# The order of loads, clamps, exponentials and score products in the head of an attention and MLP kernel, and one clamp further on

## The chip, the core and the metric

The kernel runs on one NeuronCore of a Trainium2 chip. The core has five engines with queues of their own, each of which works through its instructions in order: TensorE (PE, matrix products; PEld is its weight load), VectorE (DVE), ScalarE (ACT), GpSimd (POOL) and SyncE (SP, which here issues nearly all DMAs). They meet through semaphores. The metric is the device time of one execution in microseconds (us), less being better; the kernel before takes 689.08 us, the median of three runs (689.06 to 689.25).

## The reference

x is 8 x 8 x 512 x 64 (batch, head, position, depth), state 8 x 8 x 32 x 64. A softmax reads the state from every position of x, another reads x from every state row; both results, side by side along the sequence, go through an MLP of width 2048 with a sigmoid-approximated GELU.

```python
scores = scale * np.matmul(x, state.transpose(0, 1, 3, 2))
a = softmax(scores)                      # with max subtracted and 1e-9 added to the sum
xread = np.matmul(a, state)
scores2 = scale * np.matmul(state, x.transpose(0, 1, 3, 2))
a2 = softmax(scores2)
sread = np.matmul(a2, x)
x = concat([xread, sread], axis=2)       # -> 4352 tokens x 512
h = x @ w_in                             # 512 x 2048
g = h * (1.0 / (1.0 + np.exp(-1.702 * h)))
return g @ w_out                         # 2048 x 512
```

(`softmax` and `concat` stand for lines written out in the reference.) All arrays are float32, but the two weights are handed over as float64.

## The kernel before

The weights' 64-bit words are loaded as they are and turned into float32 on the core, in pieces of 128 x 512 numbers: 16 pieces of w_in (piece 4c+k is the k-th block of 128 rows of column block c), then 16 of w_out. So w_in's third and fourth pieces are pieces 2 and 3, needed for the first column block; w_out's fifth is piece 20 (`nin + 4`). A piece takes these steps:

- `mask` (L221, DVE): the exponent bits of the high words.
- `round_a`: clamps the exponent to float32's range and scales it: two Relu activations on ACT (L232, L233), or for pieces 18 and 19 two `tensor_scalar` on DVE (L229, L230).
- `fraction` (L239, DVE), `sign` (L245, DVE, needs the clamped exponent), then L258 and L264 on DVE, the last writing the float32 piece.

`powers_to(n)` runs `round_a` up to piece n; `piece(fill)` finishes the next piece and puts `fill` between its two last steps; `round_to(n, ahead)` finishes all pieces up to n, each with clamps of the following ones.

The order of all work is written by hand: each engine gets its instructions in the order in which the program issues them. The head (L1295 to L1369) treats batches 0 and 1. SP's loads are issued in the order state (on ACT), pieces 0 and 1, batch 0's x in four parts, piece 2, batch 1's x in two halves (into the tile `sums`), then pieces 3 and up. Eight DMA semaphores go round, so from the ninth load on an issue waits for the landing of the one eight places before.

For each batch the head does the following. `two_states` (PE) and `state_copies` (ACT) transpose the state. `xT_part(b, j)` transposes two heads' x on PE (L356) and copies them on ACT (L357); parts 0 and 1 use x's first half, parts 2 and 3 its second. `att_scores` (L444) makes the scores of all 512 positions: for head row j, group g and half i, a 64-row by 32-column product on the array's tile given by i (rows) and j (columns), written to banks `o_0` and `o_1`. `score_copies` (ACT, L363) moves them to SBUF, `scores_back` (PE, L372) turns them, for batch 0 into the banks `held`. `head_max` and `head_sub` (DVE, L379 and L386) subtract each maximum, `head_exp` (ACT, L390) is one activation over 1024 elements a partition, `head_sum` (L402 to L405) and `head_scale` (L413) normalize on DVE, `head_back` (PE L422, ACT L423) turns back to `aT`.

`att_M` (PE L430, copied on ACT at L566) multiplies w_in's column block by the state: the state's reading and w_in become one matrix M, so that the nonlinear half is GELU of M times `aT` (`up_x`, PE L655, tile h; GELU at L644). The first `up_x` needs column block 0, that is pieces 0 to 3, and batch 0's normalized exponentials.

Much later, at 73 to 86 us, the product with w_out begins (L1552 on). It uses seven products P1 to P7 in place of eight. In the first pass (i = 0), pieces up to 17 are made, P1, second reads and M's of both batches are done, P2, one product of `up_x(1, f_early)` whose GELU goes to xn's place, `att_srT`, then `pair_sums` (sums on DVE, L1469), `round_to(nin + 4)` (pieces 18 and 19, with piece 20's clamp on ACT), `powers_to(nin + 6)`, P6 and the rest. P7 and P3 use the two banks of tile tag `h`, which the GELU of `up_x(1, f_early)` and one before must have read.

Of the kernel before, what the change touches and what calls it, by code (L numbers as in the profile page):

```python
# [20 lines left out]
def kernel(  # L21
# [194 lines left out]
    def mask(i):  # L216

        _, hi = words(i)
        sc = low[:, 2 + i % (AHEAD + 1)].bitcast(I32)
        power[i] = sc  # L220
        nc.vector.tensor_scalar(sc, hi, 0x7FF00000, None, ALU.bitwise_and)  # L221

    def round_a(i):

        if i not in power:
            mask(i)
        sc = power[i]
        if i in (NFC * NPR + 2, NFC * NPR + 3):
            nc.vector.tensor_scalar(sc, sc, most, least, ALU.min, ALU.max)  # L229
            nc.vector.tensor_scalar(sc, sc, -least, 8.0, ALU.add, ALU.mult)  # L230
            return
        nc.scalar.activation(out=sc.bitcast(FP32), in_=sc, func=AF.Relu, bias=edge[0], scale=-8.0)  # L232
        nc.scalar.activation(out=sc, in_=sc.bitcast(FP32), func=AF.Relu, bias=edge[1], scale=-1.0)  # L233

    def fraction(i):

        key = PIECES[i]
        dst = w_in[key[1]][:, key[2]] if key[0] == "i" else w_out[:, key[1]]
        nc.vector.tensor_scalar(dst.bitcast(I32), words(i)[1], 0xFFFFF, 0x100000, ALU.bitwise_and, ALU.bitwise_or)  # L239
        begun[i] = dst  # L240
# [32 lines left out]
    def load_weights(upto):  # L273
        while done["load"] < min(upto, len(PIECES)):
            load_weight(done["load"])
            done["load"] += 1

    def powers_to(n):
        while done["a"] < min(n, len(PIECES)):
            load_weights(done["a"] + 1)  # L280
            round_a(done["a"])
            done["a"] += 1
# [15 lines left out]
    def piece(fill):  # L298

        i = done["b"]  # L300
        powers_to(i + 1)
        round_b(i, i + 1, False, fill)
        done["b"] += 1
        refill()
# [27 lines left out]
    def state_copies(b):  # L332
        for t, ps in zip(A[b]["two"], A[b]["turn"]):
            nc.scalar.copy(t, ps)
# [10 lines left out]
    def xT_part(b, j, bank=None):  # L345

        if j == 0:
            A[b]["xT"] = apool.tile([P, H, 2, P], FP32, tag="xT", name=f"xT_{b}")
        h = slice(NG * j, NG * (j + 1))
        if bank is None:  # L350
            ps = att_ps([P, NG, 2, P], f"xT_{b}_{j}")
        else:
            ps = bank.rearrange("p (g i q) -> p g i q", g=NG, i=2)
        for g in range(NG):
            for i in range(2):
                nc.tensor.transpose(ps[:, g, i], x_pair(b, NG * j + g, i), ident)  # L356
        nc.scalar.copy(A[b]["xT"][:, h], ps)  # L357
# [8 lines left out]
    def scores_back(b, i, bank):  # L366

        ps = bank.rearrange("p (k g m) -> p k g m", k=2, g=NG)
        for k in range(2):
            for g in range(NG):  # L370
                o = P * (2 * g + k)
                nc.tensor.transpose(ps[:, k, g], A[b]["s"][i][:, o : o + P], ident)  # L372

    def head_max(b, i, banks):
        a = A[b]
        if i == 0:
            a["e1"] = apool.tile([P, SCH, NG, NPR, Ns], FP32, tag="e1", name=f"e1_{b}")
            a["mx"] = apool.tile([P, NG, NB], FP32, tag="mx", name=f"mx_{b}")
        nc.vector.reduce_max(out=a["mx"][:, i], in_=banks[i].rearrange("p (k n) -> p k n", n=Ns), axis=AX.X)  # L379

    def head_sub(b, i, banks):
        a = A[b]
        t = a["e1"].rearrange("p (k i) g j n -> p i k (g j) n", i=2)[:, i]
        ps = banks[i].rearrange("p (k m n) -> p k m n", k=2, n=Ns)
        mx = a["mx"][:, i].rearrange("p (k m) -> p k m", k=2)
        nc.vector.tensor_tensor(out=t, in0=ps, in1=mx.to_broadcast((P, 2, NB // 2, Ns)), op=ALU.subtract)  # L386

    def head_exp(b):
        t = A[b]["e1"]
        nc.scalar.activation(out=t, in_=t, func=AF.Exp, scale=scale)  # L390

    def head_sum(b, *fills):
# [39 lines left out]
    def att_scores(b):  # L432
        a = A[b]
        a["s"] = bank_o[:NG] if b < 2 else bank_o[NG:]
        if b > 1:
            by_state(b, a["s"], lambda rows, j: a["xT"][rows, j])
            return

        for g in range(NG):
            for j in range(NPR):  # L440
                st = slice(Ns * j, Ns * (j + 1))
                for i in range(2):
                    rows = slice(D * i, D * (i + 1))
                    nc.tensor.matmul(  # L444
                        a["s"][i][st, 2 * P * g : 2 * P * (g + 1)], state_of(b, NG * j + g, i),
                        a["xT"][rows, NG * j + g], start=True, stop=True,
                    )
# [120 lines left out]
    def att_M(b, c, spare=False, banks=None, copied=True):  # L568

        m = mpool.tile([P, NG, FC], FP32, tag=f"M{turns['M'] % NFC if b < 2 else c}", name=f"M_{b}_{c}")  # L570
        turns["M"] += 1
        A[b]["M", c] = m
        name = f"M_{b}_{c}_"
        ps = banks or [
            psH.tile([P, FC], FP32, tag="h", name=name + str(g)) if spare else att_ps([P, FC], name + str(g)) for g in range(NG)
        ]
        by_state(b, ps, lambda rows, j: w_in[c][rows, j])
        M_banks[b, c] = ps
        if copied:
            M_copies(b, c)  # L580
# [714 lines left out]
    load_two_states()  # L1295
    load_weights(2)
    load_x(0)
    load_weights(3)
    load_x(1)
    load_weights(2 * NPR)  # L1300
    nc.scalar.activation(out=one, in_=one, func=AF.Exp)
# [8 lines left out]
    keep_warm(3, held[0])  # L1310
    for j in range(NPR):
        xT_part(0, j, apart[j - 2] if j > 1 else None)
    piece(lambda: mask(2))
    powers_to(3)
    att_scores(0)
    fraction(2)
    score_copies(0)
    two_states(1, [apart[i][:, :P] for i in range(2)])
    state_copies(1)
    xT_part(1, 0)  # L1320
    scores_back(0, 0, held[0])
    piece(None)
    head_max(0, 0, held)
    mask(3)
    head_sub(0, 0, held)
    xT_part(1, 1)
    apart = [psH.tile([P, FC], FP32, tag="h", name=f"apart_{i}") for i in (2, 3)]
    xT_part(1, 2, apart[0])
    xT_part(1, 3, apart[1])
    scores_back(0, 1, held[1])  # L1330
    powers_to(NPR)
    att_scores(1)
    head_max(0, 1, held)
    fraction(3)
    head_sub(0, 1, held)
    score_copies(1)
    head_exp(0)
    apart = [psH.tile([P, FC], FP32, tag="h", name=f"apart_{i}") for i in (4, 5)]
    for i in range(2):
        scores_back(1, i, apart[i])  # L1340
# [120 lines left out]
    def pieces(t, *shape):  # L1461
        n, k = shape
        return t.rearrange("p a b -> p (a b)").rearrange("p (n k t) -> p n k t", n=n, k=k)
# [7 lines left out]
    def four(t):  # L1471
        return t.rearrange("p a b -> p (a b)").rearrange("p (n t) -> p n t", t=HS)
# [80 lines left out]
    for i in range(HF):  # L1553
        round_to(nin + 2 * i + 2)
        gelus(len(waiting))
        if i == 3:
            nc.scalar.copy(G[1, f_early // 2][:, f_early % 2], early)
        if i == 0:
            pair(i, "P1")
            att_sread(1)  # L1560
            att_M(1, 2, banks=bank_o[1::2])
            att_sread(0)
            att_M(1, 3, True)
            pair(i, "P2")
            f_early = rest.pop(0)
            early = xn[0].rearrange("p h c d -> p (h c d)")[:, :S]
            up_x(1, f_early, dst=early)
            att_srT(0)
            att_srT(1)
            t_room.append(pieces(apool.tile([P, NG, SCH * P], FP32, tag="eT", name="t_room_1"), 2, 2))  # L1570
            s_rooms.append(four(apool.tile([P, NG, NB * Ns], FP32, tag="e1", name="s4_room")))
            pair_sums(i)
            round_to(nin + 4)
            powers_to(nin + 6)
            pair(i, "P6")
            ps7["P7"], ps7["P3"] = (psH.tile([P, FC], FP32, tag="h", name=f"down_{k}") for k in (7, 3))
            ps7["P4"], up_bank = (att_ps([P, FC], f"down_{k}") for k in (4, "up"))
        else:
            pair_sums(i)
            pair(i, "P1", "P2")  # L1580
        if i == 2:
            G[1, f_early // 2] = free.pop(0)
        if i > 1 and i % 2 == 0:
            up_x(1, rest.pop(0), bank=up_bank, wait=True)
        if i == HF - 1:
            k1 = s_rooms[0][:, :2]
            nc.scalar.copy(k1, ps7["P1"].rearrange("p (r n) -> p r n", r=2))
        late()
        if i > 1 and i % 2:
            up_x(1, rest.pop(0), bank=up_bank if i < HF - 1 else bank_o[0], wait=True)  # L1590
        if i == HF // 2 + 1:
            load_state(2)
            load_x_squares(2)
# [140 lines left out]
```

## Time and the profile before

| | us |
|---|---|
| median of three runs | 689.08 (689.06 to 689.25) |
| the profiled execution | 688.99 |
| its span, first to last instruction | 687.2 |
| PE busy / DVE busy / ACT busy in the span | 677.6 / 558.0 / 327.9 |
| clock granted to PE | 0.998 of full |

| stretch, us from the start | length | PE busy | DVE busy | ACT busy | DMA GB/s |
|---|---|---|---|---|---|
| 0 to 8 | 8 | 6.20 | 2.42 | 3.79 | 245 |
| 8 to 16 | 8 | 7.37 | 6.82 | 7.34 | 378 |
| 16 to 24 | 8 | 6.50 | 7.86 | 5.25 | 408 |
| 24 to 32 | 8 | 7.98 | 7.72 | 7.13 | 301 |
| 32 to 40 | 8 | 8.00 | 8.00 | 7.91 | 2 |
| 60 to 120 | 60 | 60.00 | 57.33 | 38.03 | 117 |

The span is the time between the first and the last instruction on the core; what the execution takes beyond it (1.8 us) lies around it. A busy time is the union of an engine's instructions. Matmul ends are modelled, so a PE that is busy all the time is without gaps, which is not the same as working at its peak.

### The profile page before, as it was taken

How to read it: one execution, taken by the hardware profiler on the slowest of the kernel's cores; microseconds unless marked ns; L12 is line 12 of the kernel's file. 1: busy time of each engine (PE TensorE's matmuls, PEld its weight loads, DVE VectorE, ACT ScalarE, POOL GpSimd, SP SyncE). 2: the span in 40 equal slices, each digit the busy share in tenths (PEclk: the TensorE clock that was granted, in tenths of full speed). 3: DMA queues.
4: the chain of work that ended last, by engine and by line, in shares of the span. 5: the costliest groups of instructions: out<-in, count | busy, mean ns of one | idle time of the engine just before them, and what ended most of it. 6: DMA issues, size and time to landing. Idle time of an engine off the chain costs nothing.

```text
span 687.2 us, 13616 instructions
## 1 busy us (share of the span) xinstructions
PE 677.6 (99%) x5355; PEld 578.7 (84%) x5355; DVE 558.0 (81%) x1066; ACT 327.9 (48%) x725; POOL 1.5 (0%) x10
## 2 busy tenths in 40 slices
PE   8999999999999999999999999999999999999996
PEld 4443687769989999889988998899988998999995
DVE  6999899999998886988878796888698885986540
ACT  7799744134355533752375335544375237421410
POOL 0000000000000000000000000000000000000000
PEclk9999999999999999999999999999999999999999
DMA  9731245338262764156443745176415640251000
GB/s 318 302 105 49 93 140 147 116 119 270 89 156 78 208 192 113 32 166 190 151 67 112 205 144 113 32 208 192 115 27 170 187 152 1 77 169 47 2 3 29
DMA packets 100159, 87.39 MB, mean 127 GB/s; under 512 B 56576, under 2 KB 79616, under 8 KB 100096
## 3 DMA queue, kind: packets, MB, share of 16 engines
q1 hardware_dynamic: 99552, 86.40, 42.6%
q8 instruction: 42, 0.69, 0.4%
q10 hardware_dynamic: 544, 0.13, 0.1%
q14 instruction: 21, 0.17, 0.1%
HBM read 68.94 MB, written 17.56 MB: 126 GB/s over the span
## 4 chain that ended last, share of the span: by engine, by line
PE 94%; DMA 2%; DVE 2%; ACT 1%; issue 0%; DVEq 0%; ACTq 0%
PE low L802 28%; PE o L1212 15%; PE o L802 15%; PE upx L1212 6%; PE o L1539 4%; PE M L430 4%; PE down L1539 3%; PE o L655 3%; PE h L655 3%; PE o L701 3%; PE upw L1212 2%; PE o L851 2%; PE down_up L655 1%; PE o L430 1%; PE sr L622 1%; PE upx_sr L1212 1%
## 5 line engine op out<-in xcount | busy, mean ns | idle before, releaser
L802 PE MATMUL low<-w_out,g_room 128*128 128x128 f32 x416 | 54.3, 276 | 0.0
L802 PEld LDWEIGHTS low<-w_out,g_room 128*128 128x128 f32 x416 | 50.5, 192 | 4.5 <-issue 4.2
L1212 PE MATMUL o<-ta,M 128*128 128x256 f32 x192 | 49.9, 382 | 0.0
L1212 PE MATMUL upx<-aT,M 128*128 128x256 f32 x192 | 49.4, 380 | 0.0
L802 PE MATMUL low<-low,g_room 128*128 128x128 f32 x336 | 43.3, 275 | 0.0
L1212 PEld LDWEIGHTS o<-ta,M 128*128 128x128 f32 x192 | 35.5, 190 | 6.0 <-ACT g_room L1258 1.6
L802 PEld LDWEIGHTS low<-low,g_room 128*128 128x128 f32 x336 | 40.3, 192 | 0.0
L1212 PEld LDWEIGHTS upx<-aT,M 128*128 128x128 f32 x192 | 36.0, 190 | 4.8
L1218 ACT ACTIVATE g_room<-o 128x512 f32<-128x512 f32 (+1 forms) x56 | 31.4, 560 | 10.7 <-PE o L1212 10.7
L802 PE MATMUL low<-sums,later 128*128 128x128 f32 x272 | 34.9, 275 | 0.0
L566 ACT COPY M<-M 128x512 f32<-128x512 f32 x53 | 27.5, 596 | 15.2 <-PE M L430 15.2
L802 PEld LDWEIGHTS low<-sums,later 128*128 128x128 f32 x272 | 32.7, 192 | 0.1
L858 DVE TENSOR_TENSOR g_room<-g_room 128x512 f32<-128x512 f32 x48 | 31.8, 686 | 0.2
L1212 PE MATMUL o<-ta,ms 128*128 128x256 f32 x120 | 30.8, 379 | 0.0
L232 ACT ACTIVATE low<-low,edge 128x512 f32<-128x512 int32 x30 | 21.8, 726 | 17.6 <-DVE low L221 17.6
L1258 ACT COPY g_room<-o 128x512 f32<-128x512 f32 (+1 forms) x28 | 15.6, 556 | 25.0 <-PE o L1212 25.0
L1218 ACT ACTIVATE g_room<-g_room 128x512 f32<-128x512 f32 (+1 forms) x28 | 16.8, 602 | 20.8 <-DVE g_room L1221 20.8
L1212 PEld LDWEIGHTS o<-ta,ms 128*128 128x128 f32 x120 | 22.8, 190 | 3.1
L1212 PE MATMUL o<-aT,m 128*128 128x256 f32 x96 | 24.6, 379 | 0.0
L802 PEld LDWEIGHTS o<-w_out,g_room 128*128 128x128 f32 x160 | 19.4, 192 | 5.0 <-issue 5.0
L430 PE MATMUL M<-w_in,stT 64*32 64x512 f32 x344 | 23.2, 592 | 0.0
L858 DVE TENSOR_TENSOR g_room<-g_room,later 128x512 f32<-128x512 f32 x35 | 22.8, 685 | 0.0
(321 smaller groups left out, 1640.8 us busy)
## 6 DMA issues: line engine op xcount, KB each, us to landing
low<-low SPq DMA_DIRECT2D x108, 256.0 KB, 2.6
low<-low SPq DMA_DIRECT2D x11, 768.0 KB, 4.5
later<-in_moe_w_out_dram SPq DMA_DIRECT2D x16, 512.0 KB, 3.4
w_out<-in_moe_w_in_dram SPq DMA_DIRECT2D x12, 512.0 KB, 10.0
xsq<-in_x_dram SPq DMA_DIRECT2D x96, 64.0 KB, 2.3
xn<-in_x_dram SPq DMA_DIRECT2D x12, 512.0 KB, 4.2
out_dram<-osb SPq DMA_DIRECT2D x15, 256.0 KB, 2.2
out_dram<-later SPq DMA_DIRECT2D x14, 256.0 KB, 2.2
```

The lines of the kernel that those rows point to most:

```text
L232: nc.scalar.activation(out=sc.bitcast(FP32), in_=sc, func=AF.Relu, bias=edge[0], scale=-8.0)
L430: nc.tensor.matmul(ps[g][st], state_of(b, NG * j + g, g), rhs(rows, j), start=True, stop=True)
L566: nc.scalar.copy(A[b]["M", c][:, g], ps)
L655: nc.tensor.matmul(hps, lhs[i], rhs[i], start=(i == 0), stop=(i == n - 1))
L701: nc.tensor.matmul(ps[:, r], lhs[f][:, P * r : P * (r + 1)], rhs[:, f], start=(first and r == 0 and f == 0), stop=(f == HF - 1), skip_grou ...
L802: nc.tensor.matmul(ps, lhs[f], rhs[:, f], start=(first and f == 0), stop=(f == QF - 1), skip_group_check=True)
L851: nc.tensor.matmul(ps[:, r], lhs[f][:, P * r : P * (r + 1)], rhs[:, f], start=(r == 0 and f == 0), stop=(f == HF - 1), skip_group_check=True,)
L858: nc.vector.tensor_tensor(out=out, in0=x0, in1=x1, op=op)
L1212: nc.tensor.matmul(ps[:, k], lhs[i][:, o : o + P], rhs[i], start=(first and k == 0 and i == 0), stop=(i == n - 1), skip_group_check=True,)
L1218: nc.scalar.activation(out=dst, in_=src, func=AF.Gelu_apprx_sigmoid)
L1258: nc.scalar.copy(c12, Y(u))
L1539: nc.tensor.matmul(ps7[name][:, HN * r : HN * (r + 1)], lhs[:, P * r : P * (r + 1)], rhs, start=(i == 0 and r == 0), stop=(i == HF - 1), s ...
```

## The change

Seven things change; what is computed does not.

- The order of loads: piece 3 is issued ahead of batch 1's x (`load_weights(NPR)`, NPR being 4).
- Piece 2 is clamped on DVE instead of ACT, with `fraction(2)` between the two steps (`between`).
- The last step of piece 1 comes ahead of piece 2's mask (`piece(None)`).
- The score products go by j outside and g inside, for batches 0 and 1.
- Batch 0's scores are turned back as soon as each is copied, between the first parts of batch 1's x; piece 2 is finished, and piece 3 masked and its fraction taken, ahead of `head_max`; piece 3's clamp on ACT stands ahead of the copies of parts 2 and 3 of batch 1's x.
- Batch 0's exponentials are two activations of 512 elements, the first ahead of `score_copies(1)`, the second behind.
- In the first pass of w_out's product, `pair_sums` and `round_to(nin + 4, 1)` are issued ahead of P2 and `up_x(1, f_early)`. On ACT this puts piece 20's clamp ahead of that GELU and of the copies of `att_srT`; on PE and DVE the order there is as before, and the second argument changes nothing for these pieces.

```diff
--- before.py
+++ after.py
@@ -220,13 +220,15 @@
         power[i] = sc
         nc.vector.tensor_scalar(sc, hi, 0x7FF00000, None, ALU.bitwise_and)
 
-    def round_a(i):
+    def round_a(i, between=None):
 
         if i not in power:
             mask(i)
         sc = power[i]
-        if i in (NFC * NPR + 2, NFC * NPR + 3):
+        if between or i in (NFC * NPR + 2, NFC * NPR + 3):
             nc.vector.tensor_scalar(sc, sc, most, least, ALU.min, ALU.max)
+            if between:
+                between()
             nc.vector.tensor_scalar(sc, sc, -least, 8.0, ALU.add, ALU.mult)
             return
         nc.scalar.activation(out=sc.bitcast(FP32), in_=sc, func=AF.Relu, bias=edge[0], scale=-8.0)
@@ -385,8 +387,10 @@
         mx = a["mx"][:, i].rearrange("p (k m) -> p k m", k=2)
         nc.vector.tensor_tensor(out=t, in0=ps, in1=mx.to_broadcast((P, 2, NB // 2, Ns)), op=ALU.subtract)
 
-    def head_exp(b):
+    def head_exp(b, i=None):
         t = A[b]["e1"]
+        if i is not None:
+            t = t.rearrange("p (k i) g j n -> p i k (g j n)", i=2)[:, i]
         nc.scalar.activation(out=t, in_=t, func=AF.Exp, scale=scale)
 
     def head_sum(b, *fills):
@@ -436,8 +440,8 @@
             by_state(b, a["s"], lambda rows, j: a["xT"][rows, j])
             return
 
-        for g in range(NG):
-            for j in range(NPR):
+        for j in range(NPR):
+            for g in range(NG):
                 st = slice(Ns * j, Ns * (j + 1))
                 for i in range(2):
                     rows = slice(D * i, D * (i + 1))
@@ -1295,7 +1299,7 @@
     load_two_states()
     load_weights(2)
     load_x(0)
-    load_weights(3)
+    load_weights(NPR)
     load_x(1)
     load_weights(2 * NPR)
     nc.scalar.activation(out=one, in_=one, func=AF.Exp)
@@ -1310,31 +1314,31 @@
     keep_warm(3, held[0])
     for j in range(NPR):
         xT_part(0, j, apart[j - 2] if j > 1 else None)
-    piece(lambda: mask(2))
-    powers_to(3)
+    piece(None)
+    round_a(2, lambda: fraction(2))
+    done["a"] = 3
     att_scores(0)
-    fraction(2)
     score_copies(0)
     two_states(1, [apart[i][:, :P] for i in range(2)])
     state_copies(1)
+    sign(2)
+    piece(lambda: mask(3))
+    fraction(3)
+    scores_back(0, 0, held[0])
     xT_part(1, 0)
-    scores_back(0, 0, held[0])
-    piece(None)
-    head_max(0, 0, held)
-    mask(3)
-    head_sub(0, 0, held)
+    scores_back(0, 1, held[1])
     xT_part(1, 1)
+    powers_to(NPR)
+    for i in range(2):
+        head_max(0, i, held)
+        head_sub(0, i, held)
     apart = [psH.tile([P, FC], FP32, tag="h", name=f"apart_{i}") for i in (2, 3)]
     xT_part(1, 2, apart[0])
     xT_part(1, 3, apart[1])
-    scores_back(0, 1, held[1])
-    powers_to(NPR)
     att_scores(1)
-    head_max(0, 1, held)
-    fraction(3)
-    head_sub(0, 1, held)
+    head_exp(0, 0)
     score_copies(1)
-    head_exp(0)
+    head_exp(0, 1)
     apart = [psH.tile([P, FC], FP32, tag="h", name=f"apart_{i}") for i in (4, 5)]
     for i in range(2):
         scores_back(1, i, apart[i])
@@ -1561,16 +1565,16 @@
             att_M(1, 2, banks=bank_o[1::2])
             att_sread(0)
             att_M(1, 3, True)
+            t_room.append(pieces(apool.tile([P, NG, SCH * P], FP32, tag="eT", name="t_room_1"), 2, 2))
+            s_rooms.append(four(apool.tile([P, NG, NB * Ns], FP32, tag="e1", name="s4_room")))
+            pair_sums(i)
+            round_to(nin + 4, 1)
             pair(i, "P2")
             f_early = rest.pop(0)
             early = xn[0].rearrange("p h c d -> p (h c d)")[:, :S]
             up_x(1, f_early, dst=early)
             att_srT(0)
             att_srT(1)
-            t_room.append(pieces(apool.tile([P, NG, SCH * P], FP32, tag="eT", name="t_room_1"), 2, 2))
-            s_rooms.append(four(apool.tile([P, NG, NB * Ns], FP32, tag="e1", name="s4_room")))
-            pair_sums(i)
-            round_to(nin + 4)
             powers_to(nin + 6)
             pair(i, "P6")
             ps7["P7"], ps7["P3"] = (psH.tile([P, FC], FP32, tag="h", name=f"down_{k}") for k in (7, 3))
```

## The prediction

> **What bounds the kernel now.** I read the page's first part, then the waits of TensorE (PE), once up to 24 us and once after, then the table of stretches, then the timelines of the engines up to 24 us and around 82 us. All times are us from the span's start; line numbers are those of the kernel before.
>
> ```profile
> PE 677.6 (99%) x5355; PEld 578.7 (84%) x5355; DVE 558.0 (81%) x1066; ACT 327.9 (48%) x725; POOL 1.5 (0%) x10
> ...
> PE apart L372 <- ACT sums L363: 0.8, 1, 0.8
> PE aT L422 <- DVE e L413: 0.6, 1, 0.6
> PE o L372 <- ACT sums L363: 0.2, 1, 0.2
> PE xT L356 <- DMA sums<-in_x_dram: 0.2, 1, 0.2
> ...
> 24.00:29.00 5.00, 4.99 (x12) 1.00 1.03 410
> 29.00:192.00 163.00, 162.99 (x1082) 1.00 0.40 124
> ```
>
> The stretches' columns are length, PE busy, instructions, granted clock, DMA share, GB/s. PE works without a gap from 24.01, where the first product with the nonlinear half begins (h, L655), to 192, and the view of PE's waits after 24 us names none. So the end moves with the start of that product, and only the head, up to 24 us, can change the time. The four waits in the head after the start-up are 1.8 us together: no change of the head that leaves PE's work as it is can win more than about that.
>
> What releases the h product at 24.01 is a chain over all engines:
>
> ```profile
> 10.40 1.80 PE L444 MATMUL o<-xT,two 64*32 64x256 f32 x32
> 12.74 0.63 PE L356 MATMUL xT<-ident,sums 128*128 128x128 f32 x4 [0.17 <-DMA sums<-in_x_dram]
> 15.91 1.50 PE L444 MATMUL o<-xT,two 64*32 64x256 f32 x32
> ...
> 12.96 1.05 ACT L363 COPY sums<-o 128x512 f32<-128x512 f32 x2
> 15.19 1.11 ACT L357 COPY xT<-apart 128x512 f32<-128x512 f32 x2
> 16.14 0.78 ACT L232 ACTIVATE low<-low,edge 128x512 f32<-128x512 int32 x1
> 16.95 0.72 ACT L233 ACTIVATE low<-low,edge 128x512 int32<-128x512 f32 x1
> 17.58 1.05 ACT L363 COPY sums<-o 128x512 f32<-128x512 f32 x2
> 18.52 1.07 ACT L390 ACTIVATE e<-e 128x1024 f32<-128x1024 f32 x1
> ...
> 11.11 0.43 DVE L221 TENSOR_SCALAR low<-w_out 128x512 int32<-128x512 int32 x1 [0.53 <-DMA w_out<-in_moe_w_in_dram]
> 13.09 0.69 DVE L245 SCALAR_TENSOR_TENSOR low<-w_out,low 128x512 int32<-128x512 int32 x1 [0.61 <-ACT low L233]
> 20.02 1.21 DVE L402 TENSOR_REDUCE sm<-e 128x32 f32<-128x1024 f32 x1
> ```
>
> Columns: start, time from first start to last end, engine, line, operation. VectorE (DVE) has only two waits after 9 us, 0.53 for the third piece of w_in and 0.61 for its clamp on ScalarE (ACT); otherwise its own queue leads to the sums (L402) at 20.02, which need batch 0's exponentials (end 19.59, so 0.43 of slack) and release, through L413 and the transposes L422, the h product 3.99 us later.
>
> **What the skill says.** The Trainium skill, TensorEngine Tiling (Array Packing), section Tiling Modes: different tiles of the array can work in parallel. The trace agrees, and shows the reverse as well: in the score product at 15.91 six records of three tile pairs start within 0.03 us, but the last pair of head row j=3, on the same tiles as the pair before it, comes at 16.81, 0.46 after it (16.35). TensorE: Matmul & The Clock Gate, section Part 1, says that ACT and DVE are strict FIFO, which is what the walk below rests on, and that PE falls to half clock after an idle window of about 3.4 us; the trace holds clock 1.00 through gaps of about 1.2 us at 17.0 and 21.5. DMA: Bandwidth & Descriptors, section Queues, rings and completion order: each engine consumes descriptors in ring order, so a load put ahead delays what follows. SP's later issues, which wait for these transfers, agree: they start at 11.11, 12.62, 14.06, 15.36 and 16.71, that is, w_in's third piece, x1's halves, w_in's fourth and fifth landed just before.
>
> **The change, part by part.** I walk each engine's queue in its new order. From the rows: a dependent DVE step of 512 words takes 0.69 (0.43 for a tensor_scalar), an independent next one starts 0.60 (0.34) after the start; ACT copies are 0.59 to 0.62 and follow at 0.47 to 0.49.
>
> (1) Fourth piece ahead of x1. It lands at about 11.09+1.30=12.4, 1.3 being the spacing 14.06 to 15.36. x1's first half goes from 12.6 to 13.9, its second from 14.0 to 15.3; the fifth piece stays at 16.6. SP issues it at the place that waited for w_out's first landing, and x1's two issues move one place down, to about 7.0 and 7.4, while the DMA engines are still busy with older loads: no cost of its own.
>
> (2) Third piece's clamp on DVE. ACT loses L232 and L233 (0.73+0.72), DVE gains two tensor_scalars. DVE: L264 of piece 1 at 10.61 (it no longer sits behind the load), mask 2 at 11.21, first clamp 11.67, fraction 12.01, second clamp 12.35, sign 12.81, L258 13.42, mask 3 14.02, L264 14.36, fraction 3 14.97, then max and subtraction of both halves 15.30, 16.01, 16.61, 17.32 (end 18.00), sign 3 17.92, L258 18.52, L264 19.24, so it is free for the sums at 19.85 against 20.02. Added 0.86, taken back by both waits (1.14): a gain of 0.17, if nothing else is late.
>
> (3) Scores by j, then g. Two products of one j share their tiles, and PE issues in order, so each g=1 waits for its g=0 and holds the next j. From 10.40: j0 10.40, its second 10.86, and each further j adds 0.44, so the last record starts at 12.41 and ends at 12.79 instead of 12.20. What covers this is ACT: the score copies waited for the clamp there (start 12.96) and now start at 12.82. Without (2) it would cost about 0.5.
>
> (4) Order of batch 1's x. PE: states' turn 12.72; scores_back(0,0) at 13.44, after the first copy (12.82 to 13.39); xT(1,0) at about 13.95 to 14.02, where x1's first half and the queue come together; scores_back(0,1) 14.49; xT(1,1) 14.93, ending 15.53 (before 14.67); the apart pair 15.37 to 16.4. ACT: copy of xT(1,1) 15.56 to 16.18; then, new here, the fourth piece's clamp stands AHEAD of the two apart copies: 16.05 to 16.80 and 16.83 to 17.55; apart copies 17.45 to 18.07 and 17.93 to 18.55. Before, the second of them ended at 16.30: 2.25 late. Behind the clamp wait these copies, behind them PE's scores of j=2, 3 of batch 1, and both engines' rest. Scores(1): j3 at 18.60 and, like before (16.35 to 17.41), 1.06 to its end: 19.66. Score copies 19.69 to 20.74 (before 17.58 to 18.63).
>
> (5) Exponentials in two parts. The first (512 elements) fits into ACT's wait, 18.45 to 19.05: nothing. The second stands behind the score copies: 20.63 to 21.23. No row shows this form; below it is half of 1.07, 0.54, above the 0.73 of an ACT step on 512 words in SBUF; I take 0.60, like the copies. So L402 starts at 21.25 instead of 20.02: **+1.23**. Its later chain is as before: h at 25.24. PE's own queue would be ready earlier: scores_back(1) 20.3 to 21.4, M(0,0) and M(1,0) from 21.4 to 23.3, M copies to 23.5, first transposes due at 23.9. From 24 us on all engines shift together, and the weights, fixed in time by DMA, are then earlier, not later.
>
> (6) w_out's fifth piece. ACT has it 1.9 sooner (about 80.5 to 82.0 instead of 82.43 to 83.93), removing this wait:
>
> ```profile
> 83.97 0.69 DVE L245 SCALAR_TENSOR_TENSOR low<-later,low 128x512 int32<-128x512 int32 x1 [1.92 <-ACT low L233]
> 81.64 0.60 ACT L644 ACTIVATE xn<-h 128x512 f32<-128x512 f32 x1 [1.65 <-PE h L655]
> 83.38 1.03 PE L1539 MATMUL down<-w_out,g_room 128*128 128x256 f32 x4
> ```
>
> PE is gapless there, so a faster DVE gives 0. The GELU now behind the clamp moves from 81.64 to about 82.0, ends at 82.6, and P7, whose bank it frees, starts at 83.38: hidden by 0.8. If that cover failed, it would cost at most the 0.35 by which the GELU moved. PE's order there does not change.
>
> Sum: +1.23 on a span of 687.2 and an execution of 688.99, which makes 690.2; the three runs' median, 689.08, is 0.09 above that execution, so 690.3.
>
> **The rivals.** (A, forecast) ACT's queue delays batch 1's scores: 690.3; with the form of the second exponential and 0.3 on landings and queues in doubt, 689.9 to 690.8.
> (B) Worse: PE, underfed from 16.5 to 25, drops its clock. The bf16 warm-up products took 634 ns at the start against 379 later in this trace. One window of 3.4 us (the page's figure, so an estimate) at half speed adds 1.7: 692.0. For it: longer stretches of small tiles with waits; against it: no gap over about 1.2 us, as before.
> (C, not slower) DVE stays the bound and (2) gives its gain: L402 at 19.85, 688.9. For it: DVE has the longest queue in the head now. This needs the second exponential to end by 19.85, so score copies from 18.3, scores(1) done by 18.27, the last apart copy ended by 17.2. My walk has 18.55, 1.35 too late; from a partial error of the walk anything from 688.7 to 689.6 follows.
> (D) The clamp of (6) does act, through a PE wait that the records hide: up to its 1.9, 688.4 with (A)'s loss. Against it: PE's waits after 24 us are none.
>
> **How the numbers follow.** 0.2% of 689.08 is 1.38 and is about what a measurement of this kernel can tell from no change; the bounds are 687.7 and 690.46. A 0.60 (0.34 of it within the bound, 0.26 above), B 0.14 (all above), C 0.23 (0.21 within, and 0.02 below, should nearly all of the head's 1.8 us of waits go), D 0.03 (0.02 within, 0.01 below, together with C). Faster 0.03, same 0.57, slower 0.40. The range leaves out about half of C below and half of B above: 689.0 to 691.6; the forecast's own is 689.9 to 690.8.
>
> **What would show it.** Right: clamp L232/L233 of piece 3 between batch 1's copies near 16 to 17.5, the last apart copy ending near 18.5, the second exponential after the score copies, DVE idle more than 1 us before the sums, h at about 25.2, and the same distance from there to the end. Score records of batch 0 ending near 12.8 show (3). Wrong: DVE without a wait before the sums (C), h matmuls apart by more than 0.43 (B), or a gap of PE after 25 us that before has not.

## The result, and the profile after

The changed kernel takes 690.32 us (median of 22 runs, 689.77 to 691.93) against 689.24 us for the kernel before beside it (22 runs): 1.08 us more, a ratio of 1.0019 with a 95% interval of 1.0012 to 1.0025. The span of the profiled execution went from 687.2 to 688.1 us. The forecast was 690.3.

The waits of PE in the changed kernel, up to 26 us, then the stretch after it (columns as in the prediction; line numbers are those of the changed kernel, where L448 is the score product, L358 the transpose of x, L659 the h product):

```profile
...
PE aT L426 <- DVE e L417: 0.7, 1, 0.7
PE apart L374 <- ACT sums L365: 0.7, 1, 0.7
PE xT L358 <- DMA sums<-in_x_dram: 0.5, 1, 0.5
PE o L448 <- ACT xT L359: 0.5, 1, 0.5
PE o L374 <- ACT sums L365: 0.3, 1, 0.3
```
```profile
30.00:192.00 162.00, 161.98 (x1074) 1.00 0.40 122
```

In these views PE is gapless after the head, as before. The wait for x has grown from 0.2 to 0.5, and one of 0.5 inside the score product is new. The timelines of the engines over the same steps:

```profile
10.28 1.80 PE L448 MATMUL o<-xT,two 64*32 64x256 f32 x32
...
13.88 0.63 PE L358 MATMUL xT<-ident,sums 128*128 128x128 f32 x4 [0.48 <-DMA sums<-in_x_dram]
...
16.36 1.08 PE L448 MATMUL o<-xT,two 64*32 64x256 f32 x16
17.90 1.54 PE L448 MATMUL o<-xT,two 64*32 64x256 f32 x16 [0.47 <-ACT xT L359]
...
25.11 3.27 PE L659 MATMUL h<-aT,M 128*128 128x512 f32 x7
```
```profile
15.42 0.59 ACT L359 COPY xT<-xT 128x512 f32<-128x512 f32 x1 [0.23 <-PE xT L358]
15.90 0.72 ACT L234 ACTIVATE low<-low,edge 128x512 f32<-128x512 int32 x1
16.66 0.72 ACT L235 ACTIVATE low<-low,edge 128x512 int32<-128x512 f32 x1
17.29 1.05 ACT L359 COPY xT<-apart 128x512 f32<-128x512 f32 x2
18.23 0.64 ACT L394 ACTIVATE e<-e 128x512 f32<-128x512 f32 x1
19.48 1.07 ACT L365 COPY sums<-o 128x512 f32<-128x512 f32 x2 [0.61 <-PE o L448]
20.44 0.64 ACT L394 ACTIVATE e<-e 128x512 f32<-128x512 f32 x1
```
```profile
19.16 0.69 DVE L266 SCALAR_TENSOR_TENSOR w_in<-w_in,low 128x512 f32<-128x512 f32 x1
21.11 1.22 DVE L406 TENSOR_REDUCE sm<-e 128x32 f32<-128x1024 f32 x1 [1.27 <-ACT e L394]
```

The clamp (L234, L235) stands between the second and third copy of batch 1's x; the last copies end at 18.34, PE's score product breaks off for them, the score copies follow at 19.48 and the second exponential ends at 21.08. DVE was done at 19.85 and waits 1.27 for it. The h product starts at 25.11 instead of 24.01.

The two executions did not start alike: the first score product came at 10.28 here and at 10.40 before, ahead of anything that the change touches except loads, and it varies from 10.28 to 10.67 over the runs below. I therefore compare the distance from the first score product to the first h product: 14.83 here, 13.61 before, so 1.22 more (each distance is from one profiled execution). From the h product to the product L1212 (L1216 after) that starts at 191.88 before and at 192.97 after it is 167.87 and 167.86, so up to there the whole change happens in the head.

From the h product to the end of the span it is 663.19 before and 662.99 after: about 0.2 of the loss comes back, at 564 us. First before, then after:

```profile
562.96 1.06 PE L802 MATMUL low<-low,g_room 128*128 128x128 f32 x8
563.58 0.29 DVE L807 TENSOR_TENSOR g_room<-low,g_room 128x128 f32<-128x128 f32 x1 [0.36 <-issue]
...
563.92 1.13 PE L1212 MATMUL upx<-aT,M 128*128 128x256 f32 x4
...
564.89 1.03 PE L1212 MATMUL o<-ta,ms 128*128 128x256 f32 x4
```
```profile
564.05 1.06 PE L806 MATMUL low<-low,g_room 128*128 128x128 f32 x8
564.42 0.28 DVE L811 TENSOR_TENSOR g_room<-low,g_room 128x128 f32<-128x128 f32 x1
...
564.94 1.03 PE L1216 MATMUL upx<-aT,M 128*128 128x256 f32 x4
...
565.81 1.03 PE L1216 MATMUL o<-ta,ms 128*128 128x256 f32 x4
```

Before, DVE stands idle for 0.36 ahead of this step, for nothing that the profile shows, and the product starts 0.05 after the step's end. From the PE group ahead of it (562.96 before, 564.05 after) to the one behind it (564.89 and 565.81) it takes 1.93 before and 1.76 after. PE counts as busy throughout, and the view of its waits names none here. The idle time is there in all three kernels of this study that have the third piece's clamp on ACT (663.1 to 663.2 from h to the end), and in none of the six that have it on DVE (662.9 to 663.0); the experiment that puts this clamp alone back on ACT brings it back. How two DVE steps at 12 us come to change a wait at 564 us is not shown.

### The profile page after: what moved, and what is told of

It reads as the page before. It is cut to its first block, busy times and chain, and to the rows that moved or that the text cites. A ratio compares the mean times of both kernels' runs of the same rounds, so it can differ in the third digit from the quotient of the medians.

```text
span 688.1 us, 13618 instructions
## 1 busy us (share of the span) xinstructions
PE 678.5 (99%) x5355; PEld 579.6 (84%) x5355; DVE 558.8 (81%) x1068; ACT 326.7 (47%) x724; POOL 1.4 (0%) x10
## 4 chain that ended last, share of the span: by engine, by line
PE 94%; DMA 3%; ACT 1%; DVE 1%; issue 0%; ACTq 0%; DVEq 0%
PE low L806 28%; PE o L1216 15%; PE o L806 15%; PE upx L1216 6%; PE o L1543 4%; PE M L434 4%; PE down L1543 3%; PE o L659 3%; PE h L659 3%; PE o L705 3%; PE upw L1216 2%; PE o L855 2%; PE down_up L659 1%; PE o L434 1%; PE sr L626 1%; PE upx_sr L1216 1%
## 5 line engine op out<-in xcount | busy, mean ns | idle before, releaser
L1216 PE MATMUL o<-ta,M 128*128 128x256 f32 x192 | 49.9, 382 | 0.0
L1216 PE MATMUL upx<-aT,M 128*128 128x256 f32 x192 | 49.3, 379 | 0.0
L1216 PEld LDWEIGHTS o<-ta,M 128*128 128x128 f32 x192 | 35.5, 190 | 6.0 <-ACT g_room L1262 1.6
L1216 PEld LDWEIGHTS upx<-aT,M 128*128 128x128 f32 x192 | 36.0, 190 | 4.6
L1216 PE MATMUL o<-ta,ms 128*128 128x256 f32 x120 | 30.8, 379 | 0.0
L234 ACT ACTIVATE low<-low,edge 128x512 f32<-128x512 int32 x29 | 20.9, 722 | 14.3 <-DVE low L221 14.3
L1216 PEld LDWEIGHTS o<-ta,ms 128*128 128x128 f32 x120 | 22.8, 190 | 3.1
L1216 PE MATMUL o<-aT,m 128*128 128x256 f32 x96 | 24.6, 379 | 0.0
```

Of the source, the lines that this page charges most:

```text
L1216: nc.tensor.matmul(ps[:, k], lhs[i][:, o : o + P], rhs[i], start=(first and k == 0 and i == 0), stop=(i == n - 1), skip_group_check=True,)
```

## The experiments

All run complete kernels, five rounds each, beside the kernel before on the same chip. The first four ran together, the last three on another chip; the kernel before has a mean span of 687.19 us on both (42 and 49 runs). Diffs are against the changed kernel if nothing else is said. The theory is that of the prediction: the loss comes through ScalarE's queue, in which the fourth piece's clamp stands ahead of copies that batch 1's scores need.

The spans of the single runs scatter less than their times (686.9 to 687.6 in those 91 runs of the kernel before, against 688.67 to 690.66), so they tell kernels apart that the times do not. The last column is from the one profiled execution of each:

| kernel | runs | their spans, us | mean span over that of before | first score to h, over before |
|---|---|---|---|---|
| changed | 22 | 688.0 to 688.5 | +1.07 | +1.22 |
| the clamp behind the copies | 21 | 687.4 to 688.2 | +0.48 | +0.62 |
| the loads alone, in the kernel before | 13 | 687.5 to 688.0 | +0.53 | +0.46 |
| the exponentials in one | 6 | 688.5 to 688.7 | +1.43 | +1.56 |
| loads back, clamp behind | 13 | 686.6 to 687.0 | -0.44 | -0.29 |
| the third piece's clamp on ACT again | 13 | 687.4 to 687.8 | +0.40 | +0.28 |
| loads back, clamp ahead | 21 | 687.8 to 688.3 | +0.88 | +1.01 |
| the late part and the score order back | 21 | 688.0 to 688.6 | +1.04 | +1.15 |

Where the third piece's clamp is on DVE, the span has grown by 0.11 to 0.15 less than the head; where it is on ACT, by 0.07 to 0.12 more. The difference, about 0.2, agrees with what the traces show at 564 us.

### The clamp behind the copies

```diff
-    powers_to(NPR)
     for i in range(2):
         head_max(0, i, held)
         head_sub(0, i, held)
...
     xT_part(1, 3, apart[1])
+    powers_to(NPR)
     att_scores(1)
```

> The changed kernel with one move: the fourth piece's clamp on ScalarE stands behind the copies of parts 2 and 3 of batch 1's x, instead of ahead of them. Theory (ScalarE's queue): the last of these copies ends about 1.4 us sooner (17.05 instead of 18.34), the second part of the exponentials ends near 20.45 instead of 21.08, because the clamp is now in the way of the score copies by a smaller amount; the sums start near 20.5 instead of 21.11 and the h product near 24.5 instead of 25.11; time about 0.65 us below the changed kernel, still about 0.45 above the kernel before. Rival (loads: batch 1's x lands 1.3 us later and that alone sets the head): the h product stays within 0.15 us of 25.1. Rival (VectorE's two added steps set it): no change either, and VectorE has no wait before the sums.

690.10 us against 689.44, ratio 1.0010 (1.0003 to 1.0016). ACT and DVE in this kernel's timelines:

```profile
16.27 1.07 ACT L359 COPY xT<-apart 128x512 f32<-128x512 f32 x2
17.23 0.73 ACT L234 ACTIVATE low<-low,edge 128x512 f32<-128x512 int32 x1
18.00 0.72 ACT L235 ACTIVATE low<-low,edge 128x512 int32<-128x512 f32 x1
18.62 0.61 ACT L394 ACTIVATE e<-e 128x512 f32<-128x512 f32 x1
19.14 1.05 ACT L365 COPY sums<-o 128x512 f32<-128x512 f32 x2
```
```profile
18.75 0.69 DVE L247 SCALAR_TENSOR_TENSOR low<-w_out,low 128x512 int32<-128x512 int32 x1 [0.57 <-ACT low L235]
...
20.76 1.22 DVE L406 TENSOR_REDUCE sm<-e 128x32 f32<-128x1024 f32 x1
```

The copies no longer wait, but the score copies still stand behind the clamp and the first exponential, and now DVE waits 0.57 for it. From the first score product (10.52) to h (24.75) it is 14.23: 0.60 won, 0.65 expected. Moving the clamp alone undoes half of the loss.

### The loads alone, in the kernel before

```diff
# against the kernel before
-    load_weights(3)
+    load_weights(NPR)
     load_x(1)
```

> The kernel before with one part of the change alone: w_in's fourth piece loaded ahead of batch 1's x. Rival (the loads' order makes the whole loss): h product 1.1 us later than before, near 25.1. Theory (ScalarE's queue makes the larger part): the x waits cost only part of it, since ScalarE and VectorE have slack of about 0.4 before the sums; the sums start near 20.35 instead of 20.02, h near 24.35, time 0.35 us above before (0.1 to 0.6).

689.55 us against 689.44, ratio 1.0003 (0.9995 to 1.0011): no difference that the times can tell. The spans can (0.53 more), and so can the trace. PE waits 1.39 for x instead of 0.17, and the head is 0.46 longer than before (h at 24.62, first score at 10.55), where 0.35 was expected. From the PE timeline:

```profile
14.10 0.63 PE L356 MATMUL xT<-ident,sums 128*128 128x128 f32 x4 [1.39 <-DMA sums<-in_x_dram]
```

So more than half of that wait is absorbed in the order of before, and the loads' order alone makes 0.46 of the 1.22.

### The exponentials in one

```diff
-    head_exp(0, 0)
     score_copies(1)
-    head_exp(0, 1)
+    head_exp(0)
```

> The changed kernel with batch 0's exponentials in one activation of 1024 elements behind the score copies. Theory (the end of the exponentials releases the sums and hence the h product): 1.07 instead of 0.64 stands behind the score copies, so sums and h come 0.43 us later (h near 25.5) and the time is 0.4 us above the changed kernel. Rival (something else, such as the product M with w_in or its copies, sets the h product): no change.

691.28 us against 689.44 (6 runs), ratio 1.0029 (1.0017 to 1.0040). From the DVE timeline:

```profile
21.65 1.22 DVE L406 TENSOR_REDUCE sm<-e 128x32 f32<-128x1024 f32 x1 [1.63 <-ACT e L394]
```

The sums wait 1.63 for the exponentials instead of 1.27; first score to h is 15.17, 0.34 more than with two parts, and the mean span is 0.36 more, where 0.4 was expected. (The time is 0.96 above the changed kernel's; what goes beyond 0.36 lies outside the span, in six runs.) The end of the exponentials does release the chain, and in the order of the changed kernel the split is a gain.

### Loads back, clamp behind

```diff
-    load_weights(NPR)
+    load_weights(3)
     load_x(1)
...
-    sign(2)
-    piece(lambda: mask(3))
-    fraction(3)
-    scores_back(0, 0, held[0])
     xT_part(1, 0)
+    scores_back(0, 0, held[0])
     scores_back(0, 1, held[1])
     xT_part(1, 1)
-    powers_to(NPR)
-    for i in range(2):
-        head_max(0, i, held)
-        head_sub(0, i, held)
+    sign(2)
+    piece(None)
+    head_max(0, 0, held)
+    mask(3)
+    head_sub(0, 0, held)
...
     xT_part(1, 3, apart[1])
+    head_max(0, 1, held)
+    fraction(3)
+    head_sub(0, 1, held)
+    powers_to(NPR)
     att_scores(1)
```

> The changed kernel with the loads in the order of before, mask and fraction of the fourth piece at the places they had before among the maxima and subtractions, and its clamp behind the copies of batch 1's x; the third piece's clamp on VectorE, the two-part exponentials, the score order and the late part stay. Theory (ScalarE's queue and the late x are what costs, the VectorE clamp and the split gain): last copy of x near 16.1, score copies from 17.95, exponentials done by 19.6, so VectorE is the bound again, without a wait before the sums, which start at 19.65 to 19.8; h 0.1 to 0.3 us sooner than in the kernel before (23.6 to 23.9), time 1.2 to 1.4 us below the changed kernel and 0.1 to 0.3 below before. Rival (VectorE's two added steps are a cost of 0.9 us): time about 0.6 above before. Rival (the score order or the late part costs): time stays 0.5 us or more above before with sums at the same place as before.

The edit also puts `scores_back(0, 0, ...)` behind `xT_part(1, 0)` again, as in the kernel before.

689.24 us against 689.44, ratio 0.9997 (0.9989 to 1.0006). In this kernel's timelines:

```profile
18.98 0.64 ACT L394 ACTIVATE e<-e 128x512 f32<-128x512 f32 x1
...
19.80 1.21 DVE L406 TENSOR_REDUCE sm<-e 128x32 f32<-128x1024 f32 x1
...
23.79 3.70 PE L659 MATMUL h<-aT,M 128*128 128x512 f32 x8
```

The exponentials end at 19.62, DVE has no wait before the sums, and from the first score product (10.47) to h it is 13.32: 1.51 less than in the changed kernel and 0.29 less than before. In the trace it is ahead of both kernels; in time, its interval lies below the changed kernel's, while it can't be told from the kernel before. The spans tell it: 0.44 less than the kernel before.

### The third piece's clamp on ACT again

```diff
# against the kernel with loads back and clamp behind
-    round_a(2, lambda: fraction(2))
-    done["a"] = 3
+    powers_to(3)
+    fraction(2)
```

> The kernel of the experiment with loads back and clamp behind, with the third piece's clamp on ScalarE again (two Relu activations, fraction behind them in the order). Theory (the VectorE clamp is a gain, as it takes 1.45 us out of ScalarE's queue ahead of the score copies): score copies start near 13.1 instead of 12.3, VectorE waits about 1.2 us for the clamp, the sums start 0.35 us later, h comes 13.65 us after the first score product instead of 13.32, time 0.35 us above that kernel. Rival (the two added VectorE steps cost more than they save, VectorE being the bound): the sums start sooner, up to 0.5 us.

689.57 us against 689.27, ratio 1.0002 (0.9994 to 1.0011). First score to h is 13.89, 0.57 more than with the clamp on DVE, where 0.33 was expected; the wait in the DVE timeline is the one expected:

```profile
13.48 0.69 DVE L247 SCALAR_TENSOR_TENSOR low<-w_out,low 128x512 int32<-128x512 int32 x1 [1.21 <-ACT low L235]
```

Two steps more on DVE, which bounds the head there, are a gain in that order, since ACT's two steps stood ahead of the score copies and DVE waited for them. The timelines part the 0.57. That wait makes 0.41 of it: the sign step L247 starts 2.81 after the first score product (13.48 and 10.67) instead of 2.40 (12.87 and 10.47). The fourth piece's sign step, behind a clamp that ends at 18.52, brings it to 0.48 (7.88 instead of 7.40), and the sums, behind exponentials that end at 20.53, to 0.56 (9.89 instead of 9.33).

### Loads back, clamp ahead

The kernel with loads back and clamp behind, with `powers_to(NPR)` ahead of parts 2 and 3 of x.

```diff
# against the kernel with loads back and clamp behind
+    powers_to(NPR)
     apart = [psH.tile([P, FC], FP32, tag="h", name=f"apart_{i}") for i in (2, 3)]
...
     head_sub(0, 1, held)
-    powers_to(NPR)
```

> The kernel of the experiment with loads back and clamp behind, with the fourth piece's clamp ahead of the copies of parts 2 and 3 of batch 1's x, as in the changed kernel: so the changed kernel with the loads of before. Theory (ScalarE's queue is the seat of the loss and the loads' order only adds where the queue leaves room): the clamp waits for the mask of a piece that lands at 15.2, holds the copies until 17.3, and the last of them ends near 18.3 as in the changed kernel; h 14.6 us after the first score product (14.83 in the changed kernel, 13.32 in the kernel with the clamp behind), time 1.2 us above that kernel. Rival (late x is the seat): h at most 0.6 us later than with the clamp behind.

690.15 us against 689.27, ratio 1.0014 (1.0008 to 1.0021); first score to h 14.62, 1.30 more than with the clamp behind. The ACT and PE timelines:

```profile
15.96 0.72 ACT L234 ACTIVATE low<-low,edge 128x512 f32<-128x512 int32 x1 [0.57 <-DVE low L221]
16.72 0.72 ACT L235 ACTIVATE low<-low,edge 128x512 int32<-128x512 f32 x1
17.35 1.05 ACT L359 COPY xT<-apart 128x512 f32<-128x512 f32 x2
...
17.96 1.54 PE L448 MATMUL o<-xT,two 64*32 64x256 f32 x16 [1.31 <-ACT xT L359]
```

x is there early, PE has its first half of the scores done at once, and then waits 1.31 for copies that stand behind the clamp. The clamp itself waits 0.57 for the mask, which DVE makes at 15.51, without a wait, behind the first maximum; the piece landed just before, as SP's issue that waits for it, at 15.49, shows. Four kernels make a square (distance from the first score product to h; 13.61 in the kernel before):

| | clamp ahead of the copies | clamp behind |
|---|---|---|
| fourth piece ahead of x | 14.83 (the changed kernel) | 14.23 |
| x ahead of the fourth piece | 14.62 | 13.32 |

Either cause alone keeps most of what lies between 13.32 and 14.83: 1.30 with the clamp, 0.91 with the loads. With the clamp ahead, the order of loads matters 0.21; with it behind, 0.91. The rows differ in more than the loads: DVE's mask and fraction of the fourth piece and PE's first `scores_back` moved with them, and no run undoes these alone. What the traces show of the loads is PE's wait for x, 0.46 with the clamp behind and the fourth piece first, and none with x first.

### The late part and the score order back

```diff
-        for j in range(NPR):
-            for g in range(NG):
+        for g in range(NG):
+            for j in range(NPR):
...
             att_M(1, 3, True)
-            t_room.append(pieces(apool.tile([P, NG, SCH * P], FP32, tag="eT", name="t_room_1"), 2, 2))
-            s_rooms.append(four(apool.tile([P, NG, NB * Ns], FP32, tag="e1", name="s4_room")))
-            pair_sums(i)
-            round_to(nin + 4, 1)
             pair(i, "P2")
...
             att_srT(1)
+            t_room.append(pieces(apool.tile([P, NG, SCH * P], FP32, tag="eT", name="t_room_1"), 2, 2))
+            s_rooms.append(four(apool.tile([P, NG, NB * Ns], FP32, tag="e1", name="s4_room")))
+            pair_sums(i)
+            round_to(nin + 4)
             powers_to(nin + 6)
```

> The changed kernel with two parts undone: the score products by g outside and j inside again, and the late part (sums and rounding of w_out's pieces) behind P2 and the early up product again, so the fifth piece's clamp is behind that GELU. Theory: both parts were worth nothing in time. The score product of batch 0 again ends 1.8 us after its start, since its last pair needs four record slots of 0.22 us after part 3 of x in either order; VectorE waits about 1.9 us for the clamp near 85 us again while TensorE stays gapless; time within 0.2 us of the changed kernel. Rival (the prediction's step, a busy tile of the array holds all later products): the changed kernel had lost 0.6 us in each score product, and batch 0's score product ends sooner here by that much. Rival (the late part gains or costs): TensorE shows a gap near 80 to 90 us in one of the two, and the time differs by 0.4 to 1.9 us.

690.19 us against 689.27, ratio 1.0015 (1.0008 to 1.0021), like the changed kernel's 1.0019; first score to h 14.76, 0.07 less. DVE's wait for the late clamp is back, and PE's P7 (down) stands where it does in the changed kernel (84.48 there). Batch 1's score product shows why the new order did not help: here 8 records instead of 16 run ahead of the copies, but the 24 behind them take the same 1.54. From the timelines of DVE and PE:

```profile
85.07 0.69 DVE L247 SCALAR_TENSOR_TENSOR low<-later,low 128x512 int32<-128x512 int32 x1 [1.90 <-ACT low L235]
...
84.49 1.03 PE L1543 MATMUL down<-w_out,g_room 128*128 128x256 f32 x4
...
10.39 1.80 PE L448 MATMUL o<-xT,two 64*32 64x256 f32 x32
...
17.94 1.54 PE L448 MATMUL o<-xT,two 64*32 64x256 f32 x24 [0.91 <-ACT xT L359]
```

Both parts are worth nothing, the score order in the head (0.07) and the late part behind it (less than 0.1 from h to the end), and batch 0's score product takes 1.80 in either order.

No run undoes, by itself, the last step of piece 1 ahead of the third piece's mask, or the two-part exponentials in another order than the changed kernel's; what these are worth is not shown.

## Why the prediction was right, and where it was not

The sum was 1.23, the head grew by 1.22; the forecast 690.3 met 690.32. That it met it within 0.02 is luck in part. The forecast started from 689.08, but the kernel before took 689.24 beside the changed one, 0.16 more; and the time grew by 1.08, 0.15 less than the sum. The claim that only the head can change the time, since PE has no gap behind it up to 192 us, was not quite right: it had nothing for the 0.2 at 564 us. The steps, from (2) on with 0.12 taken off the forecast times for the earlier start:

- (1) Landings. SP's issues that wait for them start at 12.26, 13.77, 15.24 and 16.59; 12.4, 13.9, 15.3 and 16.6 had been forecast. Right.
- (2) DVE's walk. DVE was free for the sums at 19.75 to 19.85, forecast 19.73. That moving the clamp to DVE gains was confirmed by putting it back, in the kernel with loads back and clamp behind (0.57); in the changed kernel, where DVE waits 1.27 before the sums, it was not put back.
- (3) Scores by j, then g. **Wrong.** The step said that each g=1 holds every later product because its tile is busy, and that the product ends 0.6 later. It took 1.80 us in both orders. (A record is one entry of the trace; the 16 products of a batch leave 32, two each.) The view of the tile `two` between 10.3 and 10.9 in the changed kernel shows why:

```profile
L448 PE MATMUL o<-xT,two x18: 376/376/400, 10.3 to 10.8; 64*32 64x256 f32 x18
```

By 10.8, 18 records had started; with the held queue of that step it would have been eight. So, as the records run, a product whose tile is busy does not hold those of other tiles. The score copies came at 12.11 instead of 12.70. I had read a hold into the last pair of the order of before, which was only the one that had nothing left beside it.

- (4) ACT's queue. The two apart copies were forecast at 17.33 to 18.43 and came at 17.29 to 18.34; the score copies at 19.57, and came at 19.48. Right, and the square shows that the clamp's place is needed for the full loss: with the clamp behind, 0.62 of the 1.22 is left. But PE came to the transposes of x for another reason than step (4) took first: its queue was there 0.48 early, because (3) had not happened, and waited for x. The step had x and the queue come together at 13.95 to 14.02; with the false term gone, x alone set that time, and the sum stayed. That the false term did no harm was luck; whether it would have gone into the sum had x landed earlier, no run shows.
- (5) The half exponential took 0.64 (taken: 0.60); the sums came at 21.11, forecast 21.13, and h at 25.11, forecast 25.12. One activation instead of two costs 0.34 more.
- (6) The late clamp. DVE's wait of 1.92 went and nothing was won, as forecast. Its price was mis-sized: the GELU did not move by 0.35 but by nothing (82.73, which is 81.64 plus the 1.1 of the head), since the clamp's mask comes earlier than the one I had taken for it and the clamp was over at 82.45:

```profile
81.73 0.72 ACT L235 ACTIVATE low<-low,edge 128x512 int32<-128x512 f32 x1
...
82.73 0.60 ACT L648 ACTIVATE xn<-h 128x512 f32<-128x512 f32 x1 [0.28 <-PE h L659]
```

Of the rivals, (B), the clock, did not come: records of h are 0.43 apart and the granted clock is 1.00. (The gaps of about 1.2 us that the prediction names at 17.0 and 21.5 are distances between the starts of records; PE's waits there are the 0.8 and 0.6 of the view.) (C), DVE as the bound, is the state that, of the kernels with the third piece's clamp on DVE, only the one with loads back and clamp behind reaches; it is worth 0.29 there (13.32 against 13.61), where (C) had 0.17 at the sums. (D), that the late clamp acts through a hidden PE wait, fell with the experiment on the late part; a loss that PE's waits do not name does exist, but at 564 us.

## What to carry to other kernels

Where engines work their queues in order, the price of a step moved is read from what stands behind it on its engine: here a clamp of two steps of 0.72 us stood ahead of copies that PE needed sooner than VectorE needed the clamp. Two causes that delay the same step hide each other, so undo them singly and together before one is called harmless. And a wait that vanishes on an engine off the path, such as the 1.92 us at 84 us, is worth nothing where TensorE has no gap. The reverse does not hold: a view of waits that names none is no proof that no time is lost, as the 0.2 at 564 us shows. Compare the distance between two fixed products as well.

## What the runs showed of the hardware

Float32 products on separate tiles of the array (64 rows by 32 columns, 256 columns moving) ran side by side even where the order puts two for the same tile next to each other: the twelve products of three head rows (24 records) took four slots of about 0.22 us in the changed kernel, the first 18 records starting within 0.52 us (10.28 to 10.80). A wait on a semaphore did hold later products: with the score order back, only 8 records of batch 1's score product ran ahead of a wait of 0.91 for x's copies (17.94), while by j, then g, with the same x in place, 16 did. Whether the array or the translation of the program puts the records in that order, the runs do not show.
